# A convolution kernel stored by lag modulo 128, so that its Toeplitz rows are read in runs of 2 KB

## The chip, the core and the metric

The kernel runs on one core of a Trainium2 chip. The time is device microseconds (us) of one execution. The matrix engine is called PE in the profile and its weight loads PEld; VectorE is DVE, ScalarE is ACT, GpSimd is POOL, and SyncE, which issues most DMAs here, is SP. Five instruction streams run side by side and wait for each other on semaphores.

## The reference

Two branches work on the same sequence `x` of 2048 positions by 512 channels, and a gate mixes them:

```python
g = sigmoid((x * gate_w).sum(-1, keepdims=True))
a = attention(x, wqkv, wo)            # 32 heads of 16, full softmax over 2048 keys
b = ssm(x, ...)                       # see below
return g * a + (1 - g) * b
```

The second branch makes for each of the 512 channels a convolution kernel of 2048 taps from 128 complex modes, `K[d, l] = Re(sum_n C[d,n] * dt*B[d,n] * exp(dt*A[d,n] * l))`, and convolves the channel with it causally, `y[d, t] = sum_l K[d, l] * u[d, t - l]`, plus `u * Dskip`. (The reference does it with an FFT; the kernel does not.) Inputs and output are bf16.

## The kernel before, in words

**Attention** sets the rhythm. It is cut into 2048 score tiles of 128 keys by 512 queries. Three tiles make a group, 683 groups in all, numbered here from 0. For each group PE makes the scores (`SC<-Qm,KT`), ACT takes the exponential of them in one instruction (`ET<-SC`, 1536 columns wide), and PE multiplies the result with the values (`OA<-ET,VE`). From group 206 on, DVE takes one tile of many groups by a trick on the bits (`DZ<-SC`, then `DU`), so that ACT's instruction is 1024 columns wide there. Two score buffers, SC0 and SC1, alternate: PE can make the scores of one group while ACT works on the other.

**The second branch** is fitted into what the attention leaves of PE, DVE and the DMA queues, in this order:

- `params`: DVE makes powers of each mode's base, `L1`, `L2`, ..., by squaring. `POW` lists them.
- `tables`: for 8 slices (w) of 64 channels DVE makes two tables. The taps are a product of a 32-entry table `AT` and a 64-entry table `PL`, so that 32 x 64 = 2048 lags come from 96 entries. Thread `tables` may start after the mark "A" (the powers for `AT`), and needs "B" (those for `PL`) from its middle on.
- `kgen`: PE multiplies the tables (`MB<-PL,AT`, 2048 small matmuls), DVE moves the taps to `Ks`, and SP stores `Ks` to DRAM (`gm_kd<-Ks`). A slice is stored by 4 DMAs of 64 KB, one for each 16 channels.
- `relay`: `x` is transposed and written to DRAM as `xr`, in 16 planes (position modulo 16).
- `cloads`: for each of the 32 units of 16 channels SP loads the weights `WT` (4 DMAs of 256 KB from `gm_kd`) and the inputs `U` (2 DMAs of 284 and 288 KB from `gm_xr`). A row of `WT` is a Toeplitz row: row p + 1 is the same taps as row p, one lag further. Three buffers of each take turns.
- `convs`: 128 matmuls for each unit (`MB<-U,WT`): for 16 channels, 8 blocks of 128 lags. The weights of one matmul are 32 values per partition, taken from `WT` with a step; four matmuls lie side by side in four column strips of the array. DVE moves the result to `Ys`.
- `turn`: after two units, matmuls with a 0/1 matrix `sel` (`MB<-sel,Ys`) bring the result from 32 rows per channel back to positions.
- `gate`: the 44 small sums of the gate, in three parts of 12, 16 and 16, with matmuls of a single column (`MB<-gwT,xT`).
- `projs`: the projections of the attention (`MB<-Wv,xT`, `MB<-xT,Wk`, `MB<-xT,Wq`).

All of these share one bank of PSUM, `MB`, and lock it in turn.

**What sets the order.** A planner (`Sched`) runs when the kernel is built: threads offer their next piece with an estimated cost, and the piece that fits in before the next exponential is written into the engines' streams. It also puts in matmuls with zeros (`OA<-wm`, `SC<-wm`, `MB<-wm`) where PE would do too little. So any change of the work of one thread can shift the pieces of all others; on the chip each engine then works strictly in the order written.

Of the kernel before, what the change touches and what calls it, by code (L numbers as in the profile page):

```python
# [28 lines left out]
NPAD = 16  # L29
VB = (S + NPAD) * 16  # L30
# [53 lines left out]
POW = (1, 2, 4, 8, 16, 32, 48, 256, 512, 1024)  # L84
# [373 lines left out]
def declare(nc, es):  # L458
# [60 lines left out]
    for m in (4, 8, 512, 1024):  # L519
        sb(f"F{m}", 3 * D)  # L520
# [118 lines left out]
def record(nc, p, B, ins):  # L639
# [453 lines left out]
    def params():  # L1093
# [23 lines left out]
        for m in (4, 8):  # L1117
            yield from square(f"L{m}", f"L{m // 2}")
            yield from factor(f"F{m}", f"L{m}", key(f"L{m}"))
        for k, m in enumerate((16, 32)):  # L1120
            yield from square(f"L{m}", f"L{m // 2}")
            yield from factor("FF", f"L{m}", key(f"L{m}"), 3 * D * k)
        yield from fmul("L48", 1, "L16", key("L16"), "L32", key("L32"))
        yield from factor("FF", "L48", [(B["L48"], (0, "m"))], 6 * D)
# [49 lines left out]
    def tables():  # L1174
        AB, BS, FF = B["AB"], B["BS"], B["FF"]
        yield ("AFTER", "A")
        for w in range(8):
# [40 lines left out]
    dma("SP", lambda e: e.dma_start(kd.dram(S * 16, [[VB, 32], [1, 256]]), wm(0, [[1, 256]], 0, 32)), [(wm, 0)], [(kd, "z")], c=.6, lat=3)  # L1218

    def kgen(w):  # L1220
# [4 lines left out]
        for b in range(2):  # L1225
# [14 lines left out]
            op("DVE", lambda v, b=b: v.tensor_copy(ks(8 * b, [[16, 64], [1, 8]]), MB(0, [[1, 64], [64, 8]])), ky, [(ks, b, w)], c=.62)  # L1240
            sch.unlock("MB")
        sch.mark(f"kg{w}")
        for j in range(4):
# [1 line left out]
            dma("SP", lambda e, j=j: e.dma_start(kd.dram((4 * w + j) * VB, [[1024, 32], [1, 1024]]), ks(0, [[1, 1024]], 32 * j, 32)),
                [(ks, 0, w), (ks, 1, w)], [(kd, 4 * w + j)], c=.6, lat=3)
# [25 lines left out]
    def cloads():  # L1272
        yield ("AFTER", "xr")
        yield ("AFTER", CLAT)
        for x in range(NU_):
            v = x // UPV
            wt, ut = B[f"WT{v % NWT}"], B[f"U{x % NU}"]
            if x % UPV == 0:
# [3 lines left out]
                nb = 16 // WSP  # L1282
                for i in range(WSP):
                    yield ("SP", .65)
                    pc, sub = divmod(i, WSP // PC)
                    bigload(lambda e, pc=pc, sub=sub, i=i, wt=wt, v=v: e.dma_start(wt(NT * 16 * (PC * nb * sub + pc), [[NT * 16 * PC, nb], [1, NT * 16]]),
                                                                   kd.dram(v * VB + (16 // PC * pc + nb * sub) * 128 * 16, [[16, P], [128 * 16, nb], [1, NT * 16]])),
                            [(kd, v), (kd, "z")], [(wt, i, v)], 2 * NT * 16 * nb * P / 1000)
# [376 lines left out]
```

## Time and profile before

| | us |
|---|---|
| median of 3 timed runs | 792.45 (790.75 to 793.37) |
| the profiled execution, its own time | 790.26 |
| its span, first to last instruction | 788.5 |
| ACT busy in it | 764.4 |
| DVE busy | 698.6 |
| PE busy (ends of matmuls are modelled) | 706.7 |
| granted PE clock, mean | 0.992 |

The page gives busy times, the chain of work that ended last, and groups of instructions; the trace can also be asked for stretches of time (busy time of each engine, granted clock, DMA share) and for an engine's instructions in order of time, with the idle time ahead of each in brackets and what ended it. "issue" means that the engine waited for nothing that the profile shows. In DMA listings q1 is the queue of the data transfers and q8 and q14 carry instructions to the engines.

### The profile page before, as it was taken

To read this page: it belongs to the slowest core of one execution; us is meant where nothing else is said; L and a number is where in the kernel's file an instruction comes from. 1 tells how busy PE (TensorE), PEld (TensorE's weight loads), DVE (VectorE), ACT (ScalarE), POOL (GpSimd) and SP (SyncE) were. 2 spreads that over 40 slices of the span, in tenths; PEclk is the share of its full clock that TensorE was granted. 3 is DMA by queue.
4 is the path that set the end of the run, shared out by engine and by line. 5 is a ranking of instruction groups with operands and counts; after the bars stand their busy time and mean duration, and the time that the engine had idled before them with its cause. 6 is when DMAs were issued, how large, how long until landed. Compare 5 with 4: busy or idle time off the path is not lost.

```text
span 788.5 us, 31097 instructions
## 1 busy us (share of the span) xinstructions
PE 706.7 (90%) x14262; PEld 323.0 (41%) x14262; DVE 698.6 (89%) x1078; ACT 764.4 (97%) x694; POOL 11.9 (2%) x21
## 2 busy tenths in 40 slices
PE   6778777899899989999999999999999999998996
PEld 2323322454454544434444444444444444442221
DVE  5799999999899978878797988999989999999995
ACT  5999999999999999999999999999999999999995
POOL 4000000000000000000000000000000000000000
PEclk8999999999999999999999999999999999999999
DMA  9463000000100036003665555477554556304011
GB/s 213 84 127 63 9 5 20 24 25 26 30 25 26 26 100 162 13 19 86 171 176 157 150 160 166 143 196 207 159 163 131 145 167 173 88 7 124 32 35 35
DMA packets 125923, 76.22 MB, mean 97 GB/s; under 512 B 34240, under 2 KB 116576, under 8 KB 125792
## 3 DMA queue, kind: packets, MB, share of 16 engines
q1 hardware_dynamic: 123776, 73.05, 35.1%
q8 instruction: 112, 1.84, 1.0%
q10 hardware_dynamic: 2016, 1.18, 0.7%
q14 instruction: 19, 0.16, 0.1%
HBM read 59.12 MB, written 10.63 MB: 88 GB/s over the span
## 4 chain that ended last, share of the span: by engine, by line
ACT 84%; PE 12%; DVE 2%; POOL 1%; issue 1%; ACTq 0%; POOLq 0%
ACT ET L949 84%; PE SC L655 5%; PE OA L655 4%; PE MB L655 3%; POOL VE L723 1%; DVE DZ L985 1%; DVE OT L1020 0%; DVE DZ L996 0%; DVE Ys L1331 0%; ACT fo L1627 0%; DVE sel L1305 0%; DVE KT L749 0%; DVE YJ L1353 0%; ACT ea L1098 0%; DVE OnT L1039 0%
## 5 line engine op out<-in xcount | busy, mean ns | idle before, releaser
L949 ACT ACTIVATE ET<-SC 128x1024 bf16<-128x1024 f32 (+1 forms) x683 | 756.4, 1456 | 6.3 <-PE SC L655 5.1
L655 PE MATMUL SC<-Qm,KT 32*128 32x512 bf16 x2048 | 277.9, 385 | 63.8 <-ACT ET L949 58.7
L985 DVE TENSOR_SCALAR DZ<-SC 128x512 uint16<-128x512 f32 x384 | 255.8, 684 | 41.4 <-PE SC L655 38.9
L655 PEld LDWEIGHTS SC<-Qm,KT 32*128 32x128 bf16 x2048 | 71.4, 91 | 244.7 <-ACT ET L949 209.7
L655 PE MATMUL OA<-ET,VE 128*32 128x512 bf16 x1664 | 166.0, 391 | 0.2 <-ACT ET L949 0.2
L655 PE MATMUL OA<-wm 128*32 128x512 bf16 (+3 forms) x742 | 156.8, 366 | 1.7 <-DVE wm L706 1.2
L655 PEld LDWEIGHTS MB<-U,WT 128*32 128x32 bf16 x4096 | 91.4, 153 | 32.3 <-issue 22.6
L655 PE MATMUL MB<-U,WT 128*32 128x128 bf16 (+7 forms) x4096 | 103.3, 229 | 1.5 <-issue 1.5
L655 PEld LDWEIGHTS OA<-ET,VE 128*32 128x32 bf16 x1664 | 42.5, 93 | 93.2 <-issue 91.7
L996 DVE TENSOR_SCALAR DZ<-DZ 128x2048 uint16<-128x2048 uint16 x96 | 65.6, 683 | 7.9 <-PE OA L655 7.7
L655 PE MATMUL MB<-PL,AT 128*32 128x64 bf16 (+1 forms) x2048 | 68.9, 278 | 0.1
L996 DVE TENSOR_SCALAR DU<-DZ 128x2048 uint16<-128x2048 uint16 x96 | 64.5, 685 | 0.5
L655 PEld LDWEIGHTS MB<-PL,AT 128*32 128x32 bf16 x2048 | 56.1, 139 | 11.5 <-issue 5.7
L1043 DVE TENSOR_TENSOR PL<-PL,FF 128x2048 bf16<-128x2048 bf16 x48 | 56.2, 1217 | 0.3
L655 PEld LDWEIGHTS OA<-wm 128*32 128x32 bf16 (+2 forms) x742 | 40.3, 97 | 9.1 <-issue 7.3
L655 PE MATMUL OA<-DZ,VE 128*32 128x512 bf16 x384 | 38.0, 386 | 0.0
L655 PE MATMUL OA<-DZ,VS 128*32 128x512 bf16 x384 | 37.8, 383 | 0.0
L655 PE MATMUL OA<-DU,VS 128*32 128x512 bf16 x384 | 37.7, 383 | 0.0
L1020 DVE STREAM_TRANSPOSE OT<-OA 128x512 f32<-128x512 f32 x32 | 22.7, 709 | 5.2 <-PE OA L655 5.1
L1331 DVE CAST Ys<-MB 128x512 bf16<-128x512 f32 x32 | 21.7, 679 | 0.4 <-PE MB L655 0.2
L655 PE MATMUL MB<-Wv,xT 128*32 128x128 bf16 x1024 | 19.4, 219 | 0.0
L655 PEld LDWEIGHTS MB<-Wv,xT 128*32 128x32 bf16 x1024 | 16.7, 97 | 4.0 <-issue 1.1
(133 smaller groups left out, 449.2 us busy)
## 6 DMA issues: line engine op xcount, KB each, us to landing
WT<-gm_kd SPq DMA_DIRECT2D x128, 256.0 KB, 3.5
U<-gm_xr SPq DMA_DIRECT2D x32, 288.0 KB
U<-gm_xr SPq DMA_DIRECT2D x32, 284.0 KB
gm_xr<-Xp SPq DMA_DIRECT2D x4, 576.0 KB, 5.5
gm_kd<-Ks SPq DMA_DIRECT2D x32, 64.0 KB, 1.6
gm_yn<-YJ SPq DMA_DIRECT2D x2, 1024.0 KB, 4.8
Yl<-gm_yn SPq DMA_DIRECT2D x2, 1024.0 KB, 10.6
gm_qd<-Qs SPq DMA_DIRECT2D x15, 128.0 KB, 1.7
```

The costliest lines, as they stand in the source:

```text
L655: op("PE", lambda t: t.matmul(out(), lhsT(), rhs(), start=start, stop=stop, skip_group_check=True, **kw), R, W, c=c, lat=.15, a=a, cfg=cfg)
L723: op("POOL", lambda g, pi=pi: g.memset(VE(pi * 4 * VG, [[1, 4 * VG]]), 1.0), [(idb, 0)], [(VE, (pi, k)) for k in range(16)], c=2.3)
L949: op("ACT", lambda a: a.activation(ET(512 * e, [[1, 512 * n]]), sc(0, [[1, 512 * n]]), AF.Exp, scale=DH ** -0.5), [(sc, i, g) for i in ran ...
L985: op("DVE", lambda v: v.tensor_scalar(z.u16(512 * k, [[1, 512 * n]]), sc(512 * na, [[1, 512 * n]]), XS, XB, ALU.mult, ALU.add), [(sc, na + ...
L996: op("DVE", lambda v: v.tensor_scalar(t.u16(0, [[1, 2048]]), z.u16(0, [[1, 2048]]), float(STEP[k][0]), None, ALU.add), R, W, c=.07 + 2048 ...
L1020: op("DVE", lambda v: v.transpose(OT(512 * w, [[1, 512]]), OA(0, [[1, 512]])), [(OA, 0, b)], [(OT, w, b)], c=.64)
L1043: op(eng, lambda v: v.tensor_tensor(o(), a(), b_(), f), R, W, c=c)
L1331: op("DVE", lambda v_, ys=ys: v_.tensor_copy(ys(64, [[YW, NT // 4], [1, NJ]]), MB(0, [[NJ, NT // 4], [1, NJ]])), ky, [(ys, 0, x)], c=.62)
```

## The change

The taps of a channel block lie in DRAM in another order, and everything that makes or reads them follows.

- **Storage.** Before, lag l of 16 channels lay at `16 * l`. A Toeplitz row was read as 16 pieces of 512 B, from 16 places 4 KB apart, and rows lay 32 B apart. Now lag l lies at `256 * (l % 128) + 16 * (l // 128)`: 16 blocks of lags and 16 channels for one lag modulo 128 are 512 B in one place, and the next lag modulo 128 follows. A Toeplitz row of 16 lags is now 8 KB in one place; the four loads take 2 KB of each row. Rows lie 512 B apart.
- **Wrapping round.** Rows near the end run past lag modulo 128 = 127, so 16 more entries are stored behind: the first 16 again, moved on by one block of 128 lags. That is a second small store for each 16 channels, 32 in all (`gm_kd<-Ks 16x1x240`). The DMA of zeros at the start is reshaped for the same end.
- **Exponents traded.** The table with 64 entries now covers lags modulo 128 in a way that fits the storage, the one with 32 entries the rest: `POW`, the names `F...` and the two places in `params` are exchanged. The number and shape of the instructions stay, their order does not: the powers for `AT` and the mark "A" come first now, those for `PL` and "B" after them.
- **Weights of the convolution.** The 32 values per partition were 16 elements (32 B) apart in `WT`; now they are 128 elements (256 B) apart. The 32 result rows of a channel come out in another order (even and odd in place of two halves), and `sel` is made for that.

```diff
-VB = (S + NPAD) * 16
+VB = (P + 16) * 256
-POW = (1, 2, 4, 8, 16, 32, 48, 256, 512, 1024)
+POW = (1, 2, 16, 32, 64, 128, 256, 512, 1024, 1536)
...
-        sch.mark("B")
-        yield from square("LA", "L32", 0, 0)
+        yield from square("LA", "L2", 0, 0)
...
-        for m in (512, 1024):
+        for m in (32, 64):
             yield from square(f"L{m}", f"L{m // 2}")
             yield from factor(f"F{m}", f"L{m}", key(f"L{m}"), conj=True)
         sch.mark("A")
+        for m in (128, 256):
+            yield from square(f"L{m}", f"L{m // 2}")
+            yield from factor(f"F{m}", f"L{m}", key(f"L{m}"))
+        for k, m in enumerate((512, 1024)):
...
+        sch.mark("B")
...
-            op("DVE", lambda v, b=b: v.tensor_copy(ks(8 * b, [[16, 64], [1, 8]]), MB(0, [[1, 64], [64, 8]])), ky, [(ks, b, w)], c=.62)
+            op("DVE", lambda v, b=b: v.tensor_copy(ks(8 * b, [[16, 16], [256, 4], [1, 8]]), MB(0, [[4, 16], [1, 4], [64, 8]])), ky, [(ks, b, w)], c=.62)
...
+            yield ("SP", .6, 2)
+            dma("SP", lambda e, j=j: e.dma_start(kd.dram((4 * w + j) * VB + P * 256, [[1024, 4], [256, 4], [1, 240]]), ks(16, [[256, 4], [1, 240]], 32 * j, 4)),
+                [(ks, 0, w), (ks, 1, w)], [(kd, ("x", 4 * w + j))], c=.6, lat=3)
...
-                    bigload(lambda e, pc=pc, sub=sub, i=i, wt=wt, v=v: e.dma_start(wt(NT * 16 * (PC * nb * sub + pc), [[NT * 16 * PC, nb], [1, NT * 16]]),
-                                                                   kd.dram(v * VB + (16 // PC * pc + nb * sub) * 128 * 16, [[16, P], [128 * 16, nb], [1, NT * 16]])),
-                            [(kd, v), (kd, "z")], [(wt, i, v)], 2 * NT * 16 * nb * P / 1000)
+                    bigload(lambda e, n=n, i=i, wt=wt, v=v: e.dma_start(wt(n * i, [[1, n]]), kd.dram(v * VB + n * i, [[256, P], [1, n]])),
+                            [(kd, v), (kd, ("x", v)), (kd, "z")], [(wt, i, v)], 2 * n * P / 1000)
...
-                           lambda g=g, c=c, wt=wt: wt(512 * (nb - 1 - g) + NT * hf + c, [[16, 32]]),
+                           lambda g=g, c=c, wt=wt: wt(16 * (nb - 1 - g) + NT * hf + c, [[128, 32]]),
```

**How the order moves.** The counts of instructions on ACT, DVE and POOL are the same as before, and so are their shapes but for `Ks<-MB`. PE has 20 more matmuls, all with zeros. From group 289 to the end the streams of PE are the same in kind and order; the planner's shift lies ahead of that. The first place is SP around the first load of `WT`. Before (`Ks_145` and `Ks_146` are the two buffers of taps, `U_150` and `WT_147` the first buffers of inputs and weights):

```order
L1245 DMA gm_kd<-Ks_145 32x1024 x4
L1286 DMA WT_147<-gm_kd 128x4x256 x4
L1295 DMA U_150<-gm_xr 128x1x1152
L1295 DMA U_150<-gm_xr 128x1x1136
L1286 DMA WT_148<-gm_kd 128x4x256 x2
L769 DMA Qm<-gm_qd 16x512 x4
L1286 DMA WT_148<-gm_kd 128x4x256 x2
```

Now, at the same place:

```order
L1244 DMA gm_kd<-Ks_145 32x1024
L1247 DMA gm_kd<-Ks_145 16x1x240
L1461 DMA gm_qd<-Qs 128x512
L1244 DMA gm_kd<-Ks_145 32x1024
L1247 DMA gm_kd<-Ks_145 16x1x240
L1287 DMA WT_147<-gm_kd 128x1024 x4
L1295 DMA U_150<-gm_xr 128x1x1152
L1295 DMA U_150<-gm_xr 128x1x1136
L1287 DMA WT_148<-gm_kd 128x1024 x2
L768 DMA Qm<-gm_qd 16x512 x4
L1287 DMA WT_148<-gm_kd 128x1024 x2
```

Each store of taps has a small one behind it, and each load of weights has the same size in 128 runs where it had 512. The order of `WT`, `U` and `Qm` among each other is the same.

The second place is PE where the gate's single-column matmuls stand. Before, the first two parts of the gate (14 pieces of 8 matmuls) run together in groups 203 to 226, ahead of the last `kgen`; the end of the thinnest stretch, groups 216 to 219:

```order
L655 MATMUL SC<-Qm,KT 128x512
L655 MATMUL OA<-wm 128x512
L655 MATMUL SC<-Qm,KT 128x512 x2
L655 MATMUL OA<-ET,VE 32x512 x4
L655 MATMUL SC<-Qm,KT 128x512 x3
L655 MATMUL MB<-gwT,xT 128x1 x8
L655 MATMUL MB<-wm 32x448 x4
L655 MATMUL SC<-Qm,KT 128x512 x3
L655 MATMUL MB<-gwT,xT 128x1 x8
L655 MATMUL MB<-wm 32x448 x4
L655 MATMUL SC<-Qm,KT 128x512 x3
L655 MATMUL OA<-ET,VE 32x512 x4
```

Now the last `kgen` runs straight on to group 221, the gate's first part stands in groups 230 to 239, and two units of the convolution (groups 242 to 248) come ahead of its second part (250 to 262) and third (264 to 276). The end of the first part:

```order
L654 MATMUL SC<-Qm,KT 128x512 x3
L654 MATMUL MB<-gwT,xT 128x1 x8
L654 MATMUL MB<-wm 32x448 x4
L654 MATMUL SC<-Qm,KT 128x512 x3
L654 MATMUL SC<-wm 32x512 x8
L654 MATMUL SC<-Qm,KT 128x512 x3
L654 MATMUL OA<-ET,VE 32x512 x4
L654 MATMUL SC<-Qm,KT 128x512
L654 MATMUL OA<-wm 128x512
L654 MATMUL SC<-Qm,KT 128x512 x2
L654 MATMUL OA<-ET,VE 32x512 x4
L654 MATMUL OA<-DZ_61,VE 32x512 x4
L654 MATMUL MB<-U_150,WT_147 32x128 x4
```

So the stretch of single-column matmuls is cut in two, with convolution matmuls between. The second of the two (to group 263) ends with the same rows as the stretch before.

More of the change, by code (lines that the diff above doesn't have):

```diff
@@ L28 @@
 NJP = NJ + JX
-NPAD = 16
-VB = (S + NPAD) * 16
+VB = (P + 16) * 256
 HALF_PI = math.pi / 2
@@ L518, in declare @@
     sb("BS", 4 * 2 * D)
-    for m in (4, 8, 512, 1024):
+    for m in (32, 64, 128, 256):
         sb(f"F{m}", 3 * D)
@@ L1116, in params @@
         op("DVE", lambda v: v.tensor_copy(BS(0, [[1, 4 * D]]), ZW(0, [[1, 4 * D]])), zk, [(BS, 0)], c=1.15)
[L1117 to L1124, printed above, removed]
-        sch.mark("B")
-        yield from square("LA", "L32", 0, 0)
+        yield from square("LA", "L2", 0, 0)
         yield from square("LA", "LA", 2 * D, 0)
         yield from fmul("LA", 1, "LA", [(LA, 0)], "LA", [(LA, 2 * D)], 2 * D, at=4 * D)
-        yield from square("L256", "LA", 0, 2 * D)
+        yield from square("L16", "LA", 0, 2 * D)
         al = [(LA, 0), (LA, 2 * D), (LA, (4 * D, "m"))]
-        yield from fmul("AB", 3, "LA", al, "L256", key("L256"), conj=True, at=8 * D, t=("LT1", "LT2"))
-        for k, (x, xk, n, at) in enumerate(((LA, al, 3, 0), (B["L256"], key("L256"), 1, 6 * D))):
+        yield from fmul("AB", 3, "LA", al, "L16", key("L16"), conj=True, at=8 * D, t=("LT1", "LT2"))
+        for k, (x, xk, n, at) in enumerate(((LA, al, 3, 0), (B["L16"], key("L16"), 1, 6 * D))):
             c = .07 + n * .28
@@ L1142, in params @@
         sch.mark("A")
+        for m in (128, 256):
+            yield from square(f"L{m}", f"L{m // 2}")
+            yield from factor(f"F{m}", f"L{m}", key(f"L{m}"))
+        for k, m in enumerate((512, 1024)):
+            yield from square(f"L{m}", f"L{m // 2}")
+            yield from factor("FF", f"L{m}", key(f"L{m}"), 3 * D * k)
+        yield from fmul("L1536", 1, "L512", key("L512"), "L1024", key("L1024"))
+        yield from factor("FF", "L1536", [(B["L1536"], (0, "m"))], 6 * D)
+        sch.mark("B")
     AT, PL, ct1 = [B["AT0"], B["AT1"]], [B[f"PL{k}"] for k in range(NPL)], B["ct1"]
@@ L1184, in tables @@
             ak = [(at, "one"), (at, 0)]
-            for m, n in ((8, 512), (16, 1024)):
+            for m, n in ((8, 32), (16, 64)):
                 f = B[f"F{n}"]
@@ L1198, in tables @@
             pk = [(pl, 0)]
-            for m, n in ((4, 4), (8, 8)):
+            for m, n in ((4, 128), (8, 256)):
                 f = B[f"F{n}"]
@@ L1217, in record @@
     kd = B["kd"]
-    dma("SP", lambda e: e.dma_start(kd.dram(S * 16, [[VB, 32], [1, 256]]), wm(0, [[1, 256]], 0, 32)), [(wm, 0)], [(kd, "z")], c=.6, lat=3)
+    dma("SP", lambda e: e.dma_start(kd.dram(P * 256 + 240, [[VB, 32], [256, 16], [1, 16]]), wm(0, [[16, 16], [1, 16]], 0, 32)), [(wm, 0)], [(kd, "z")], c=.6, lat=3)
     def kgen(w):
@@ L1281, in cloads @@
                     yield ("AFTER", f"cv{UPV * (v - NWT + 1) - 1}")
[L1282 removed]
+                n = 4096 // WSP
                 for i in range(WSP):
                     yield ("SP", .65)
[L1285 to L1288 removed]
+                    bigload(lambda e, n=n, i=i, wt=wt, v=v: e.dma_start(wt(n * i, [[1, n]]), kd.dram(v * VB + n * i, [[256, P], [1, n]])),
+                            [(kd, v), (kd, ("x", v)), (kd, "z")], [(wt, i, v)], 2 * n * P / 1000)
             if x >= NU:
@@ L1302, in record @@
     Ys, YJ = [B[f"Ys{k}"] for k in range(NYS)], [B["YJ0"], B["YJ1"]]
-    op("POOL", lambda g: g.iota(sid(0, [[1, 4 * NT]]), [[-1, NT], [32, 4]], base=0, channel_multiplier=-1, allow_small_or_imprecise_dtypes=True), [], [(sid, 0)], c=.2)
+    op("POOL", lambda g: g.iota(sid(0, [[1, 4 * NT]]), [[-PC, NT], [32, 4]], base=0, channel_multiplier=-1, allow_small_or_imprecise_dtypes=True), [], [(sid, 0)], c=.2)
     for k in range(PC):
-        op("DVE", lambda v, k=k: v.tensor_scalar(sel(4 * NT * k, [[1, 4 * NT]]), sid(0, [[1, 4 * NT]]), 1.0 - NT * (PC - k), None, ALU.is_equal), [(sid, 0)], [(sel, k)], c=.15)
+        op("DVE", lambda v, k=k: v.tensor_scalar(sel(4 * NT * k, [[1, 4 * NT]]), sid(0, [[1, 4 * NT]]), k - 31.0, None, ALU.is_equal), [(sid, 0)], [(sel, k)], c=.15)
     def zeros():
```

## The prediction

> **What bounds the kernel now.** I read the page's busy times first, then its chain of waits, then where ACT was idle. The page's rows for the span, for the chain by engine and by line, and for the costliest group:
>
> ```profile
> PE 706.7 (90%) x14262; PEld 323.0 (41%) x14262; DVE 698.6 (89%) x1078; ACT 764.4 (97%) x694; POOL 11.9 (2%) x21
> ...
> ACT 84%; PE 12%; DVE 2%; POOL 1%; issue 1%; ACTq 0%; POOLq 0%
> ...
> L949 ACT ACTIVATE ET<-SC 128x1024 bf16<-128x1024 f32 (+1 forms) x683 | 756.4, 1456 | 6.3 <-PE SC L655 5.1
> ```
>
> ACT is busy for 764.4 of 788.5 us, and ahead of its 683 exponentials it was idle for 6.3 us in all. The change leaves those instructions as they are, in number and width. So there is a floor: what the change can win is part of these 6.3 us, and it can lose wherever PE is late with scores for ACT. The other 18 us lie at the start and the end, which the change does not touch.
>
> So the next question is what made up the 6.3 us. ACT in order of time, the rows that carry a wait of the middle (start, length, idle time before it in brackets):
>
> ```profile
> 300.38 4.76 ACT L949 ACTIVATE ET<-SC 128x1024 bf16<-128x1024 f32 x5 [0.20 <-PE SC L655]
> 305.55 2.12 ACT L949 ACTIVATE ET<-SC 128x1024 bf16<-128x1024 f32 x2 [0.41 <-PE SC L655]
> 308.17 1.02 ACT L949 ACTIVATE ET<-SC 128x1024 bf16<-128x1024 f32 x1 [0.49 <-PE SC L655]
> 309.56 2.79 ACT L949 ACTIVATE ET<-SC 128x1536 bf16<-128x1536 f32 x2 [0.37 <-PE SC L655]
> ...
> 386.54 4.77 ACT L949 ACTIVATE ET<-SC 128x1024 bf16<-128x1024 f32 x5 [0.27 <-PE SC L655]
> 392.25 8.93 ACT L949 ACTIVATE ET<-SC 128x1024 bf16<-128x1024 f32 x8 [0.93 <-PE SC L655]
> ...
> 541.58 47.19 ACT L949 ACTIVATE ET<-SC 128x1024 bf16<-128x1024 f32 x48 [0.36 <-PE SC L655]
> 589.84 3.03 ACT L949 ACTIVATE ET<-SC 128x1024 bf16<-128x1024 f32 x3 [1.07 <-PE SC L655]
> ```
>
> Two kinds. The first four (1.47 us) lie in the gate's stretch. The last four (2.63 us) lie among the convolutions. Before 280 us there is none. The first kind, by stretches of 2 us (PEclk is the granted clock):
>
> ```profile
> 304.00:306.00 2.00, 2.00 (x22) 0.90 (x21) 1.97 (x5) 1.59 (x3) 0.00 (x0) 0.74 0.57 151
> 306.00:308.00 2.00, 2.00 (x19) 0.34 (x15) 1.13 (x2) 1.60 (x2) 0.00 (x0) 0.50 0.90 238
> 308.00:310.00 2.00, 2.00 (x26) 0.99 (x23) 1.80 (x3) 1.47 (x2) 0.00 (x0) 0.91 0.97 221
> ```
>
> The clock was halved for about 3.4 us at the end of the gate's single-column matmuls, where PE has little to do; scores then came late. The waits of 0.41, 0.49 and 0.37, 1.27 us together, are its price.
>
> The second kind: the four "issue" steps of the chain of waits among the convolutions, then PE in order of time at the last of them, then what the DMA queues moved around it (one listing before 586 us, one after), and the page's row for the whole span:
>
> ```profile
> 385.21 0.56 issue
> ...
> 390.22 0.73 issue
> ...
> 540.46 0.66 issue
> ...
> 588.11 1.04 issue
> ...
> 587.46 0.65 PE L655 MATMUL MB<-U,WT 128*32 128x80 bf16 x25
> 589.15 0.33 PE L655 MATMUL MB<-U,WT 128*32 128x96 bf16 x7 [1.04 <-issue]
> ...
> q1 hardware_dynamic: 1316, 0.66, 46.4%
> ...
> q1 hardware_dynamic: 707, 0.35, 69.4%
> q8 instruction: 1, 0.02, 4.4%
> ...
> q8 instruction: 112, 1.84, 1.0%
> ```
>
> PE stopped for 1.04 us between two matmuls of one set of four (25 is no multiple of four), where nothing is left to wait for but its own next instructions. From 580.8 to 586 us the instruction queue moved nothing while weights ran through; one packet came between 586 and 588, just ahead of the stop. The other three steps stand right ahead of the waits at 386.54, 392.25 and 541.58. The 112 packets for 2 x 14262 instructions of PE make 255 for each. My reading: PE's instructions come over the same DMA engines, 256 at a time, and behind loads of `WT` and `U` a packet comes too late. The profile shows this order of events, not the cause.
>
> **The change, part by part.** The sum is made against the profiled execution's own 790.26 us. The median of the timed runs is 792.45, so 2.2 us are added at the end.
>
> *Weights with a step of 256 B.* No row has that step. The nearest, loads of 32 columns by group, and one run of the convolution:
>
> ```profile
> L655 PEld LDWEIGHTS MB<-U,WT x4096: 135/157/180, 357.0 to 706.7; 128*32 128x32 bf16 x196
> L655 PEld LDWEIGHTS MB<-PL,AT x2048: 131/137/162, 144.0 to 338.7; 128*32 128x32 bf16 x187
> L655 PEld LDWEIGHTS OA<-ET,VE 128*32 128x32 bf16 x1664 | 42.5, 93 | 93.2 <-issue 91.7 <-ACT ET L949 0.5 <-DVE OT L1020 0.5
> 581.82 0.54 PEld L655 LDWEIGHTS MB<-U,WT 128*32 128x32 bf16 x28 [0.23 <-issue]
> ```
>
> A step of 32 B (`WT`) has a median of 157 ns, a step of 128 B (`AT`) 137, packed columns a mean of 93. So a step costs about 50 ns, and four times the step costs no more. I take 256 B as the same: 0 us. Below: if the step cost nothing, PE would gain time in which it waits for ACT anyway, 0 us. Above: 28 loads take 0.54 us, less 0.16 for the last one, so a set of four takes 0.38 / 6 = 63 ns. Twice that is 64 us more over 1024 sets. The cover is PE's own waiting among the convolutions, from 395 to 700 us:
>
> ```profile
> PEld SC L655 <- ACT ET L949: 66.2, 158, 1.2
> PE SC L655 <- ACT ET L949: 12.7, 42, 0.7
> ```
>
> 66 us of cover for some 56 us (28 of the 32 units lie there) would do on average, but the sets lie unevenly; with a quarter uncovered it would be +15 us.
>
> *Loads of 2 KB runs.* Bytes and number of DMAs stay:
>
> ```profile
> WT<-gm_kd SPq DMA_DIRECT2D x128, 256.0 KB, 3.5
> ```
>
> Nobody waits for the data: the page has no wait of PE for `WT`. What they hold up is instruction packets. Two stretches, the first with weights in 512 B runs, the second with inputs `U` in runs of 2.2 KB:
>
> ```profile
> 584.50:586.00 1.50, 1.50 (x51) 0.98 (x51) 1.50 (x4) 1.50 (x3) 0.00 (x0) 1.00 1.12 327
> 381.00:383.00 2.00, 2.00 (x67) 1.22 (x59) 0.73 (x2) 2.00 (x3) 0.00 (x0) 1.00 0.51 193
> ```
>
> The last two columns are DMA share and GB/s. At a full share 512 B runs move 327 / 1.12 = 292 GB/s and long ones 193 / 0.51 = 378. A unit's 1.05 MB of weights then take 2.8 us of the queues at best, in place of 3.2 (at 327): 0.4 us sooner, or 0.8 if rate follows share. The four stops cost ACT 0.27, 0.93, 0.36 and 1.07. With 0.4 us off each, 0 + 0.5 + 0 + 0.7 = 1.2 are left, a gain of 1.4. I take 1.3, since 40 more PE instructions (20 matmuls with zeros and their loads) shift which packet meets which load. Bounds: all four gone, -2.6; or another stop as long as the longest, +1.1.
>
> [...]
>
> *The gate moved.* The first two parts of the gate now stand apart, with two thin stretches in place of one, the second ending in the same rows as before. One halved clock costs 1.27 us. I take one again: 0. Bounds: none, -1.3; two, +1.3. The other work that moves ahead of group 289 (the last `kgen`, two units of the convolution, projections) stays the same in sum and falls where PE waits for ACT now, between 60 and 280 us:
>
> ```profile
> PEld SC L655 <- ACT ET L949: 71.0, 137, 1.0
> ```
>
> *32 more small stores.* SP issues four stores of taps in 1.7 us and four `Qm` loads behind them:
>
> ```profile
> 243.29 1.26 SPq L1245 DMA_DIRECT2D gm_kd<-Ks  x3
> 244.59 1.82 SPq L769 DMA_DIRECT2D Qm<-gm_qd  x4
> ...
> 285.45 1.70 SPq L1245 DMA_DIRECT2D gm_kd<-Ks  x4
> 287.25 2.05 SPq L1286 DMA_DIRECT2D WT<-gm_kd  x4
> ```
>
> At 0.42 us each, four more put `Qm`, loaded a block (21 groups) ahead, 1.7 us later: hidden, 0. Without that cover it would be 1.7 us for each of the three blocks whose `Qm` stands right behind such stores, +5. The exchanged exponents and `Ks<-MB` in another shape are DVE's, on which ACT does not wait ahead of group 206: 0.
>
> Sum: 790.3 + 0 - 1.3 + 0 + 0 = 789.0 as a profiled execution, 791.2 as a median.
>
> **The rivals.**
>
> - *Slow weights.* Loads at 256 B take twice as long: 790.3 + 15 + 2.2 = 807. For it: a step costs 50 ns already. Against: 32 and 128 B do not differ. It decides from about 100 ns for a set of four, where the cover runs out.
> - *A rougher middle.* Both thin stretches lose their clock (+1.3) and no stop goes away, or one more comes (+1.1): 792.7, as a median 794.9. For it: the same rows that halved the clock before now come twice near enough. Against: thin stretches elsewhere kept the clock.
> - *Nothing changes.* The stops do not hang on the length of the runs: an instruction packet gets in after a few runs of any length, or it is the loads of `U`, which stay as they are, that hold it up. For it: `U` stands behind every load of `WT`. Against: ahead of the longest stop `U` was issued only as the packet came:
>
> ```profile
> 582.56 1.46 SPq L1286 DMA_DIRECT2D WT<-gm_kd  x3
> ...
> 586.46 2.17 SPq L1295 DMA_DIRECT2D U<-gm_xr  x2
> ```
>
>   Then 790.3, as a median 792.4. [...]
> - *All of it.* The four stops and the halved clock go: 790.3 - 2.6 - 1.3 = 786.4, as a median 788.6. For it: 0.8 us off each load would end two stops and most of a third. Against: the thin stretches are two.
>
> **How the numbers follow.** Chances: forecast 0.43, nothing changes 0.19, all of it 0.15, a rougher middle 0.14, slow weights 0.09. This kernel's runs differ by 0.3%, about 2.4 us, so that is what can be told from no change. Faster than 790.1: nearly all of "all of it" and a quarter of the forecast, 0.25. Slower than 794.8: slow weights, and two thirds of the rougher middle with a little from the others, 0.20. Same: 0.55. The range is 788.0 to 796.5: it takes in all but slow weights and the far edge of the best case.
>
> **What would show it.** Right: `MB<-U,WT` loads with a median near 137 to 160 ns; "issue" steps of the chain among the convolutions shorter or fewer, with the waits behind them; ACT idle ahead of its exponentials for about 5 us; a landing time of `WT` below 3.5 us. Wrong: loads of 200 ns and more with ACT waiting for scores in each unit of the convolution; a mean granted clock below that of before (0.992); ACT waits near a store of taps.

## The result and the profile after

The changed kernel takes 813.86 us in the median (811.65 to 814.96, 4 runs), the kernel before 791.6 (790.33 to 793.37) beside it: a ratio of 1.0276, with a 95% interval of 1.0242 to 1.0310. It is slower, by 22 us, where 791.2 was forecast.

The page of the changed kernel: busy times, the chain by engine, and the groups that answer to those shown of before (behind each `x` count: busy us, mean ns of one | idle time ahead and its cause), then the landing time of `WT`:

```profile
PE 737.8 (91%) x14282; PEld 364.6 (45%) x14282; DVE 723.3 (89%) x1078; ACT 788.8 (97%) x694; POOL 11.2 (1%) x21
...
ACT 67%; PE 27%; DVE 4%; POOL 1%; issue 1%; ACTq 0%; POOLq 0%
...
L948 ACT ACTIVATE ET<-SC 128x1024 bf16<-128x1024 f32 (+1 forms) x683 | 780.9, 1454 | 8.0 <-PE SC L654 5.9
...
L654 PEld LDWEIGHTS MB<-U,WT 128*32 128x32 bf16 x4096 | 133.0, 204 | 26.4 <-issue 22.4
...
L995 DVE TENSOR_SCALAR DZ<-DZ 128x2048 uint16<-128x2048 uint16 x96 | 80.4, 838 | 7.7 <-PE OA L654 7.4
...
WT<-gm_kd SPq DMA_DIRECT2D x128, 256.0 KB, 3.1
```

The same groups on the page of the kernel before, as far as the prediction does not show them:

```profile
L655 PEld LDWEIGHTS MB<-U,WT 128*32 128x32 bf16 x4096 | 91.4, 153 | 32.3 <-issue 22.6
...
L996 DVE TENSOR_SCALAR DZ<-DZ 128x2048 uint16<-128x2048 uint16 x96 | 65.6, 683 | 7.9 <-PE OA L655 7.7
```

The span grew by 24.6 us (788.5 to 813.1). ACT was busy for 24.4 us more (764.4 to 788.8), nearly all of it in the exponentials: 683 as before, of the same widths, busy for 780.9 us where it was 756.4. Ahead of them ACT was idle for 8.0 us, 1.7 more than before; elsewhere it was idle a little less. (The mean of one, 1454 ns, did not move. ACT's instructions lie over each other, 683 times 1454 ns being 993 us, so the mean does not tell.)

Busy time alone does not say why. Most exponentials start while the one before them still runs: 661 of 682 in the kernel before, 643 in the changed one. Where scores come a little late, this overlap shrinks (it is under 0.1 us, or a gap, for 35 before and for 72 in the changed kernel), and ACT can lose time without an idle gap. The starts and ends of single exponentials in the traces separate the two. Before, one of 1024 columns that started at least 0.1 us ahead of the end of its predecessor ended 917 ns behind it, whatever ran beside it (four in five between 915 and 918); one of 1536 columns 1343 ns. So 0.1 us of overlap is enough for the scores not to count. In the changed kernel, of those that started as early, the ones of 1024 columns with more than 16 convolution loads beside them take 1018 ns on the mean, the ones with none 914. Against the pace of before, the early ones lose 16.5 us in all (0.1 before, summed over both widths): there ACT works more slowly, with its scores at hand. All others, which started late or after a gap, lose 18.8 us (9.2 before): so up to some 10 us are late scores, most of them hidden in the busy time.

DVE works more slowly too: its step in place on `DZ`, which no edit touches, went from 683 to 838 ns.

ACT by stretches, ahead of the convolutions and among them. First the kernel before, then the changed one (length, busy time and number of instructions started, granted clock, DMA share, GB/s):

```profile
0.00:320.00 320.00, 309.45 (x240) 0.98 0.27 60
320.00:720.00 400.00, 395.65 (x396) 1.00 0.49 136
```

```profile
0.00:320.00 320.00, 310.25 (x242) 0.98 0.26 60
320.00:720.00 400.00, 393.63 (x369) 1.00 0.43 132
```

Up to 320 us nothing is lost. Then, in 400 us in which ACT hardly rests in either kernel, it gets through 369 instructions for 396: 393.63 / 369 = 1.067 us for each, and 395.65 / 396 = 0.999 before. The mix of widths is nearly the same (71 of the 368 exponentials have 1536 columns, and 76 of 395 before). The granted clock is 1.00 in both. The loss begins with the convolutions, so the experiments start at their weights.

### The profile page after: what moved, and what is told of

It is laid out like the page before. It is cut to its first block, busy times and chain, and to the rows that moved or that the text cites. A ratio compares the mean times of both kernels' runs of the same rounds, so it can differ in the third digit from the quotient of the medians.

```text
span 813.1 us, 31179 instructions
## 1 busy us (share of the span) xinstructions
PE 737.8 (91%) x14282; PEld 364.6 (45%) x14282; DVE 723.3 (89%) x1078; ACT 788.8 (97%) x694; POOL 11.2 (1%) x21
## 4 chain that ended last, share of the span: by engine, by line
ACT 67%; PE 27%; DVE 4%; POOL 1%; issue 1%; ACTq 0%; POOLq 0%
ACT ET L948 67%; PE MB L654 10%; PE SC L654 9%; PE OA L654 8%; DVE DZ L984 2%; POOL VE L722 1%; DVE DZ L995 1%; DVE OT L1019 0%; DVE Ys L1331 0%; DVE DU L995 0%; DVE YJ L1353 0%; ACT fo L1627 0%; DVE sel L1305 0%; DVE VE L758 0%; DVE KT L748 0%
## 5 line engine op out<-in xcount | busy, mean ns | idle before, releaser
L948 ACT ACTIVATE ET<-SC 128x1024 bf16<-128x1024 f32 (+1 forms) x683 | 780.9, 1454 | 8.0 <-PE SC L654 5.9
L984 DVE TENSOR_SCALAR DZ<-SC 128x512 uint16<-128x512 f32 x384 | 261.8, 703 | 41.5 <-PE SC L654 40.1
L654 PE MATMUL OA<-wm 32*128 32x512 bf16 (+3 forms) x758 | 157.4, 361 | 1.2 <-DVE wm L705 1.2
L654 PEld LDWEIGHTS MB<-U,WT 128*32 128x32 bf16 x4096 | 133.0, 204 | 26.4 <-issue 22.4
L654 PE MATMUL MB<-U,WT 128*32 128x120 bf16 (+7 forms) x4096 | 138.3, 257 | 1.5 <-issue 1.5
L995 DVE TENSOR_SCALAR DZ<-DZ 128x2048 uint16<-128x2048 uint16 x96 | 80.4, 838 | 7.7 <-PE OA L654 7.4
L995 DVE TENSOR_SCALAR DU<-DZ 128x2048 uint16<-128x2048 uint16 x96 | 72.0, 764 | 0.5
L654 PE MATMUL OA<-DZ,VS 128*32 128x512 bf16 x384 | 39.9, 383 | 0.0
```

What stands on the lines that cost most here:

```text
L654: op("PE", lambda t: t.matmul(out(), lhsT(), rhs(), start=start, stop=stop, skip_group_check=True, **kw), R, W, c=c, lat=.15, a=a, cfg=cfg)
L948: op("ACT", lambda a: a.activation(ET(512 * e, [[1, 512 * n]]), sc(0, [[1, 512 * n]]), AF.Exp, scale=DH ** -0.5), [(sc, i, g) for i in ran ...
L984: op("DVE", lambda v: v.tensor_scalar(z.u16(512 * k, [[1, 512 * n]]), sc(512 * na, [[1, 512 * n]]), XS, XB, ALU.mult, ALU.add), [(sc, na + ...
L995: op("DVE", lambda v: v.tensor_scalar(t.u16(0, [[1, 2048]]), z.u16(0, [[1, 2048]]), float(STEP[k][0]), None, ALU.add), R, W, c=.07 + 2048 ...
```

## Experiments

### Which edit it is: b256, a32

> The kernel before, with only the step of the weights set to 256 B (other taps of the same tile, so the convolution sums other products; storage, transfers and order are those of before). STEP: the whole loss without any other part of the change, 810 to 816 us, loads of 204 ns, DVE's in-place step above 0.8 us while loads run. RUNS: 790 to 793. PLACE: 790 to 793.

> The kernel after, with one number undone: the 32 weights of a matmul stand 32 B apart in the same tile, as before, not 256 B. (They are other taps than those asked for, so the convolution sums other products; number and size of all instructions and DMAs are those of the kernel after.) Theory STEP: weight loads that jump 256 B hold up the memory ports for ACT and DVE and are slow themselves; then the whole loss goes, 789 to 793 us, the loads are back at 157 ns and the in-place step of DVE (DZ from DZ) at 0.68 us. Theory RUNS (the 2 KB transfers into the tiles, or the planner's shift ahead of group 289, make the loss): stays at 810 to 815. Theory PLACE (tiles lie at other addresses, so that engines collide): stays at 810 to 815.

```diff
 before.py -> b256
-wt(512 * (nb - 1 - g) + NT * hf + c, [[16, 32]])
+wt(16 * (nb - 1 - g) + NT * hf + c, [[128, 32]])
 after.py -> a32
-wt(16 * (nb - 1 - g) + NT * hf + c, [[128, 32]])
+wt(512 * (nb - 1 - g) + NT * hf + c, [[16, 32]])
```

Measured: b256 816.85 us, ratio 1.0347 (1.0285 to 1.0409); a32 789.69 us, ratio 1.0015 (0.9978 to 1.0053). The pages of b256 and of a32:

```profile
PE 739.8 (91%) x14262; PEld 365.2 (45%) x14262; DVE 724.4 (89%) x1078; ACT 789.2 (97%) x694; POOL 11.8 (1%) x21
...
L655 PEld LDWEIGHTS MB<-U,WT 128*32 128x32 bf16 x4096 | 133.7, 205 | 24.7 <-issue 20.7
```

```profile
PE 711.7 (90%) x14282; PEld 324.2 (41%) x14282; DVE 697.8 (88%) x1078; ACT 765.0 (97%) x694; POOL 11.2 (1%) x21
...
L654 PEld LDWEIGHTS MB<-U,WT 128*32 128x32 bf16 x4096 | 91.5, 153 | 32.9 <-issue 23.0
```

The step alone, put into the kernel before, brings the whole loss (ACT busy 789.2); taken out of the changed kernel it takes the whole loss away (765.0). The storage, the 2 KB runs, the extra stores, the traded exponents and the moved pieces together come to no difference that can be told. So STEP holds as far as the times go (in b256 the loads take 205 ns for 153, DVE's step in place 826 for 683), and RUNS and PLACE do not. At which point the loads hold up ACT and DVE, no run shows.

### Is it the distance: a2, a64, a128, a192, a260

> The kernel after with a step of 128 B (other taps of the same tile). STEP with a cliff between 128 and 256 B, as the tables' matmuls (128 B) let expect, beside which DVE kept its 0.68 us: 789 to 794, loads of 137 to 157 ns. STEP as a price that grows with the step: about half way, 800 to 804. RUNS or PLACE: 810 to 815.

> The kernel after with a step of 260 B: as far as 256 B, but no power of two (other taps of the same tile). If the loss at 256 B comes from falling on the same part of the memory again and again: 789 to 794. If it comes from the distance alone: 810 to 815. RUNS or PLACE: 810 to 815.

> The changed kernel with the weights read without a step (32 elements side by side, 64 B in all); the weights are then the wrong elements of the same tile, so the convolution's values are wrong, its work is the same. [...] RIVAL (a load's length in the convolution is set by the instruction and what runs beside it, not by its elements' places): 150 to 160 ns.

> The changed kernel with the weights read at a step of 64 B; the weights are then the wrong elements of the same tile, so the convolution's values are wrong, its work is the same. [...] RIVAL (only at 128 B and above is a load slowed): 157 ns and 789 to 791 us.

> The changed kernel with the weights read at a step of 192 B; the weights are then the wrong elements of the same tile, so the convolution's values are wrong, its work is the same. [...] RIVAL (what counts is the distance in multiples of 64 or 128 B, so 192 B lies between 128 B and 256 B): loads 188 to 204 ns, ScalarE busy 775 to 789 us, 800 to 812 us.

```diff
 after.py, the 32 weights of a load
-wt(16 * (nb - 1 - g) + NT * hf + c, [[128, 32]])
+wt(512 * (nb - 1 - g) + 32 * c, [[1, 32]])                          # a2
+wt(1024 * (c // 4) + 4 * (nb - 1 - g) + c % 4, [[32, 32]])          # a64
+wt(2048 * (c // 8) + 8 * (nb - 1 - g) + c % 8, [[64, 32]])          # a128
+wt(16 * (nb - 1 - g) + NT * hf + c, [[96, 32]])                     # a192
+wt((16 * (nb - 1 - g) + c) % 64, [[130, 32]])                       # a260
```

| step | load, mean ns | ACT busy, us | DVE in place, ns | ratio to before |
|---|---|---|---|---|
| none (a2; the four loads of a set begin 64 B apart) | 97 | 764.5 | 683 | 0.9977 (0.9949 to 1.0005) |
| 32 B (a32) | 153 | 765.0 | 685 | 1.0015 (0.9978 to 1.0053) |
| 64 B (a64) | 154 | 763.9 | 683 | 0.9965 (0.9940 to 0.9990) |
| 128 B (a128) | 187 | 770.9 | 685 | 1.0112 (1.0055 to 1.0169) |
| 192 B (a192) | 151 | 763.5 | 683 | 0.9978 (0.9947 to 1.0008) |
| 256 B (changed) | 204 | 788.8 | 838 | 1.0276 (1.0242 to 1.0310) |
| 260 B (a260) | 159 | 764.3 | 684 | 0.9989 (0.9960 to 1.0019) |

The page of a192, then that of a128:

```profile
L654 PEld LDWEIGHTS MB<-U,WT 128*32 128x32 bf16 x4096 | 90.7, 151 | 33.7 <-issue 23.9
```

```profile
PE 725.9 (91%) x14282; PEld 346.2 (43%) x14282; DVE 698.9 (87%) x1078; ACT 770.9 (96%) x694; POOL 11.1 (1%) x21
...
L948 ACT ACTIVATE ET<-SC 128x1024 bf16<-128x1024 f32 (+1 forms) x683 | 763.0, 1394 | 11.9 <-PE SC L654 7.6
...
L654 PEld LDWEIGHTS MB<-U,WT 128*32 128x32 bf16 x4096 | 114.6, 187 | 29.2 <-issue 22.0
```

In all rows but the first the four loads of a set begin 2 B apart. It is not the distance: 260 B costs nearly what 32 B costs, and 192 B less than 128 B. Of the steps tried, 128 B and 256 B are dear, and 32, 64, 192 and 260 B are not. With 154 ns at 64 B the RIVAL of a64 held, that only at 128 B and above a load is slowed; 192 B (151 ns) shows that "above" does not hold either.

At 128 B, 798.70 us in the median lie between what a cliff and what a price that grows with the step had let expect, and the loss is of another kind. The loads are slow, DVE keeps its 685 ns, ACT waits 5.6 us more and is busy 6.6 us more. But here an exponential of 1024 columns that started early ends 917 ns behind its predecessor, as before (four in five between 914 and 918). So ACT is not slowed: these 12.2 us are late scores, in part hidden in the busy time. A load without a step takes 97 ns and gains the kernel nothing that can be told.

### Is 256 B dear everywhere: kg256, kg32

The lag generation has 2048 loads of the same shape, at 128 B. On their row of 137 ns the prediction had leant.

> The kernel before, with the weights that make the convolution kernel's lags (tables AT, 2048 loads ahead of the convolutions) read at a step of 256 B for 128 B; they are then the wrong elements of the same tile, so the lags are wrong, the work is the same. STEP (256 B hurts whichever matmul loads so): these loads go from a median of 137 ns to 180 ns and more, VectorE's and ScalarE's instructions beside them lengthen; with half as many loads as in the convolution, 3 to 12 us longer. RIVAL (the convolution's loads are slow for a reason of that place, its moving tile or its buffers): loads stay at about 137 ns and the time within 0.3%.

> The kernel before, with the same weights read at a step of 32 B for 128 B; they are then the wrong elements of the same tile, so the lags are wrong, the work is the same. HIDDEN (at 128 B these loads are as slow in themselves as the convolution's at 128 B, and the row of 137 ns that the prediction leant on is short because of what runs beside it): the loads become shorter than 137 ns, near 100 to 120 ns. RIVAL (in this place a load's length doesn't hang on its step between 32 and 128 B): 130 to 140 ns. Either way the time within 0.3%.

```diff
 before.py, kgen
-at(AN * (k // 2) + ch, [[CH, 32]])      # CH = 64 elements, 128 B
+at(ch, [[128, 32]])                     # kg256
+at(AN * (k // 2) + ch, [[16, 32]])      # kg32
```

Measured: kg256 788.71 us, ratio 0.9984 (0.9956 to 1.0011); kg32 790.54 us, ratio 1.0005 (0.9979 to 1.0030). The page of the kernel before, of kg256 and of kg32:

```profile
L655 PEld LDWEIGHTS MB<-PL,AT 128*32 128x32 bf16 x2048 | 56.1, 139 | 11.5 <-issue 5.7
```

```profile
PE 711.0 (90%) x14261; PEld 327.9 (42%) x14262; DVE 698.2 (89%) x1078; ACT 764.2 (97%) x694; POOL 11.9 (2%) x21
...
L655 PEld LDWEIGHTS MB<-PL,AT 128*32 128x32 bf16 x2048 | 59.8, 143 | 11.8 <-issue 5.7
```

```profile
L655 PEld LDWEIGHTS MB<-PL,AT 128*32 128x32 bf16 x2048 | 59.8, 147 | 11.2 <-issue 5.7
```

My theory STEP fell here: 256 B costs these loads 143 ns, 32 B 147 ns, 128 B 139, and ACT (764.2 us busy) and DVE (698.2) do not feel it. HIDDEN fell too: the loads did not become shorter at 32 B. A step of 256 B is not dear in itself. Two things were left that differ between the places. In the convolution the four loads of a set, one for each quarter of the array's columns, begin 2 B apart (four neighbouring channels), in the lag generation 32 B apart (channel 16 * j of four). And sets follow each other faster in the convolution: worked out from the runs of loads in the trace of the kernel before, some 80 ns apart on the mean (the most usual 63), for some 114 in the lag generation.

### The four loads of a set: s256, kgline

> The changed kernel, its weights still at a step of 256 B, but the four loads of a set (four channels, one for each quarter of TensorE's columns) begin 32 B apart from each other, as those of the lag generation do, where in the changed kernel they begin 2 B apart; they read the wrong lag blocks of the same tile, so the values are wrong, the work is the same. SET (it is the four loads of a set, which run at one time, that want the same line of memory; apart, they don't collide): loads 150 to 170 ns, VectorE's in-place step 685 to 720 ns, ScalarE busy 764 to 770 us, 0.995 to 1.008 of the kernel before. RATE (each load at 256 B is slow in itself; the lag generation hides it because its moving reads hold it to a set in 113 ns for 63 ns): loads still about 204 ns, ScalarE busy about 788 us, 1.025 to 1.035.

> The kernel before, with the weights of the lag generation at a step of 256 B, and the four loads of a set 2 B apart where they were 32 B apart; they are the wrong elements of the same tile, so the lags are wrong, the work is the same. SET: these loads now collide as the convolution's do, 165 ns and more for 143 with 256 B and 32 B apart; VectorE's and ScalarE's instructions beside them lengthen; over 512 sets the time grows by 2 to 12 us. RATE: nothing moves, 140 to 150 ns, time within 0.3%.

```diff
 after.py -> s256
-wt(16 * (nb - 1 - g) + NT * hf + c, [[128, 32]])
+wt(16 * ((nb - 1 - g + c % 4) % 8) + c, [[128, 32]])
 before.py -> kgline
-at(AN * (k // 2) + ch, [[CH, 32]])
+at(4 * (ch % 16) + ch // 16, [[128, 32]])
```

Measured: s256 787.88 us, ratio 0.9975 (0.9941 to 1.0010); kgline 841.96 us, ratio 1.0682 (1.0618 to 1.0747). The loads of a set begin 34 B apart in s256 (one block of lags and one channel; 222 B where the block wraps round). The page of s256, then that of kgline:

```profile
PE 710.1 (89%) x14281; PEld 318.5 (40%) x14282; DVE 697.5 (88%) x1078; ACT 765.1 (96%) x694; POOL 11.2 (1%) x21
...
L948 ACT ACTIVATE ET<-SC 128x1024 bf16<-128x1024 f32 (+1 forms) x683 | 757.2, 1450 | 11.9 <-PE SC L654 10.4
...
L654 PEld LDWEIGHTS MB<-U,WT 128*32 128x32 bf16 x4096 | 87.0, 146 | 36.0 <-issue 25.8
...
L995 DVE TENSOR_SCALAR DZ<-DZ 128x2048 uint16<-128x2048 uint16 x96 | 65.7, 685 | 9.5 <-PE OA L654 9.3
```

```profile
PE 732.3 (87%) x14261; PEld 347.5 (41%) x14262; DVE 751.2 (90%) x1078; ACT 814.9 (97%) x694; POOL 11.9 (1%) x21
...
L949 ACT ACTIVATE ET<-SC 128x1024 bf16<-128x1024 f32 (+1 forms) x683 | 807.0, 1544 | 6.0 <-PE SC L655 4.9
...
L655 PEld LDWEIGHTS MB<-PL,AT 128*32 128x32 bf16 x2048 | 81.0, 231 | 8.2 <-issue 6.6
```

SET holds both ways as far as the times go, RATE in neither; what of the memory the four want at one time, no run shows. With the same step of 256 B the convolution's loads fall to 146 ns once the four begin 34 B apart, and DVE and ACT get their times back. The lag generation's loads rise from 143 to 231 ns once the four begin 2 B apart. That its sets follow more slowly did not save it: the 51 us that it lost are four times what I had expected at most. A stretch in which lags are made, kernel before and kgline (length; busy time and number of instructions started of PE, PEld, DVE, ACT and POOL; granted clock, DMA share, GB/s):

```profile
140.00:240.00 100.00, 91.98 (x2035) 49.70 (x2036) 91.48 (x121) 100.00 (x76) 0.00 (x0) 1.00 0.09 25
```

```profile
140.00:240.00 100.00, 80.32 (x1543) 47.61 (x1542) 94.17 (x93) 100.00 (x59) 0.00 (x0) 0.98 0.07 20
```

ACT, the fourth, gets through 59 exponentials for 76 in the same time, all of 1536 columns, and is called busy all along. It is not short of scores: of the exponentials that started early, those with more than 16 loads of the lag generation beside them take 2032 ns on the mean, for 1343 before, and that makes up the whole growth of the busy time (50.6 us).

### Does it grow with the number of such sets, and is it all: half, half2, rot

> The changed kernel with half of the convolution's weights (the second and fourth quarter of each unit's channels) read at 256 B, the others at 64 B; the latter are then the wrong elements of the same tile, so values are wrong, the work is the same. ADDITIVE (each load at 256 B takes its own share of memory time from ScalarE and VectorE): ScalarE's busy time half way, 774 to 779 us, time half way, 797 to 804 us. RIVAL (only an unbroken train of such loads starves the other engines, short ones are absorbed): ScalarE busy below 769 us, time below 795 us.

> The changed kernel with the second and fourth quarter of each unit's channels read at 256 B, the others at 64 B; the latter are then the wrong elements of the same tile, so values are wrong, the work is the same. ADDITIVE: ScalarE's busy time half way, 774 to 779 us, time half way, 797 to 804 us. RIVAL (only an unbroken train of such loads takes time from the other engines): ScalarE busy below 769 us, time below 795 us.

> The changed kernel, data, storage and step of 256 B untouched; only the order in which each of the four channels of a set goes through its lag blocks differs: the first set has block 0 for all four, as it must, and in the seven behind it each channel is one block further than its neighbour, so that their loads begin 32 B apart or a multiple of it. Everything is computed. SET: seven of eight sets no longer collide; loads at a median near 150 ns with one in eight near 200, ScalarE busy 765 to 769 us, VectorE's in-place step below 705 ns, time 0.995 to 1.004 of the kernel before. RIVAL (the matmuls of a set then have different widths and no longer end together, or the colliding eighth still costs its part, 3 us, and more): 1.004 to 1.015.

```diff
 after.py -> half2
-wt(16 * (nb - 1 - g) + NT * hf + c, [[128, 32]])
+wt(16 * (nb - 1 - g) + c, [[128, 32]]) if c // 4 % 2 else wt(1024 * (c // 4) + 4 * (nb - 1 - g) + c % 4, [[32, 32]])
 after.py -> rot (everything computed)
-for g in range(nb):
+for t in range(nb):
     ...
     for j in range(4):
+        g = 1 + (t - 1 + j) % 7 if t else 0
```

`half` did not do what it was meant to: it chose by `q % 2`, and `q` is read when the matmul is written out, after the loop has ended at 3, so that all weights stayed at 256 B. It is a second measurement of the changed kernel: 814.01 us, ratio 1.0296 (1.0251 to 1.0341). half2, which chooses by `c`: 801.44 us, 1.0134 (1.0075 to 1.0193). rot: 792.68 us, 1.0035 (1.0003 to 1.0067). The pages of half2 and of rot:

```profile
L948 ACT ACTIVATE ET<-SC 128x1024 bf16<-128x1024 f32 (+1 forms) x683 | 769.5, 1436 | 10.0 <-PE SC L654 8.3
...
L654 PEld LDWEIGHTS MB<-U,WT 128*32 128x32 bf16 x4096 | 114.4, 181 | 30.2 <-issue 23.4
```

```profile
L948 ACT ACTIVATE ET<-SC 128x1024 bf16<-128x1024 f32 (+1 forms) x683 | 760.8, 1454 | 4.0 <-PE SC L654 3.1
...
L654 PEld LDWEIGHTS MB<-U,WT 128*32 128x32 bf16 x4096 | 96.4, 158 | 31.8 <-issue 23.4
...
L995 DVE TENSOR_SCALAR DZ<-DZ 128x2048 uint16<-128x2048 uint16 x96 | 68.7, 715 | 8.6 <-PE OA L654 8.3
```

With one colliding set in eight the exponentials are busy 4.4 us longer than before (760.8 less 756.4), with one in two 13.1, with all 24.5. Over 128, 512 and 1024 sets that is 34, 26 and 24 ns each: it grows with their number, and short trains are not absorbed. rot computes everything, keeps the changed data and the 256 B step, and loses about what its eighth part explains: 4.4 us of busy time, where an eighth of 24.5 is 3.1. DVE's step in place came out at 715 ns, above the 705 that SET allowed; why a single colliding set costs more than one in a train was not looked into. So the collision is the loss.

### Versions that avoid it: fix260, fix272

> The whole change, with two elements of padding behind every 128 of a granule, in the rows that are stored, in DRAM and in the tiles WT, so that the weights of the convolution step 260 B; the wrap-around is stored by two small transfers where there was one (32 more in all). Everything is computed. [...] RIVAL (the padding, the odd pitch of the rows and the extra small transfers cost something of their own): 2 to 6 us above the kernel before, with ScalarE idle ahead of the exponentials by more than 9 us or WT landing later than 3.3 us.

> The whole change, with one element of padding behind every 16 channels (a lag takes 17 places), in the rows that are stored, in DRAM and in WT, so that the weights of the convolution step 272 B; the wrap-around stays one transfer, unlike with the padding behind every 128 places. Everything is computed. STEP: loads of a set about 152 to 158 ns, VectorE's in-place step 685 ns, ScalarE busy about 764 us; without the second wrap transfer the time is that of the other steps that cost nothing, 0.995 to 1.000 of the kernel before. RIVAL (padding and the odd pitch cost something, whatever the number of small transfers): 1.002 to 1.007, ScalarE idle ahead of the exponentials 8 us and more.

The main lines of both edits, cut:

```diff
 after.py -> fix272 (17 places for the 16 channels of a lag, everything computed)
-VB = (P + 16) * 256
+VB = (P + 16) * 272
-ks(8 * b, [[16, 16], [256, 4], [1, 8]])
+ks(8 * b, [[17, 16], [272, 4], [1, 8]])
...
-ks(16, [[256, 4], [1, 240]], 32 * j, 4)
+ks(17, [[272, 4], [1, 255]], 32 * j, 4)
...
-wt(16 * (nb - 1 - g) + NT * hf + c, [[128, 32]])
+wt(17 * (nb - 1 - g) + c, [[136, 32]])
 after.py -> fix260 (2 places behind each 128; the wrap-around in two stores)
...
-wt(16 * (nb - 1 - g) + NT * hf + c, [[128, 32]])
+wt(16 * (nb - 1 - g) + NT * hf + c, [[130, 32]])
```

Measured: fix260 792.99 us, ratio 1.0036 (1.0014 to 1.0059); fix272 787.19 us, ratio 0.9964 (0.9931 to 0.9997). The page of fix272, then that of fix260:

```profile
L948 ACT ACTIVATE ET<-SC 128x1024 bf16<-128x1024 f32 (+1 forms) x683 | 756.3, 1441 | 7.7 <-PE SC L654 6.5
...
L654 PEld LDWEIGHTS MB<-U,WT 128*32 128x32 bf16 x4096 | 89.3, 150 | 32.3 <-issue 22.3
```

```profile
L948 ACT ACTIVATE ET<-SC 128x1024 bf16<-128x1024 f32 (+1 forms) x683 | 757.0, 1406 | 9.4 <-PE SC L654 8.2
...
L654 PEld LDWEIGHTS MB<-U,WT 128*32 128x32 bf16 x4096 | 98.4, 159 | 34.0 <-issue 25.6
```

Both have the exponentials' busy time of before (756.4). fix272 is 3.0% faster than the changed kernel by the ratios (0.9964 / 1.0276 = 0.970) and 0.4% faster than the kernel before, with an interval that just leaves out 1. fix260 came out 0.4% above before, as its rival said it might: ACT idle 9.4 us and waiting for scores. The length of its loads is not enough to explain that: a260 has the same 159 ns and stands at 0.9989. Whether the 32 further small stores do it was not taken apart.

## Why the prediction was wrong, step by step

- **"... four times the step costs no more. I take 256 B as the same: 0 us."** This term of the sum failed. It was the whole loss, 24.6 us of the span: b256 shows that the step alone brings it, a32 that without it nothing is lost. The term compared 32 B in the convolution (157 ns) with 128 B in the lag generation (137 ns), as if the step were all that differs. The four loads of a set begin 2 B apart in the one and 32 B apart in the other. In the convolution itself the answer at 128 B is 187 ns (a128), and at 256 B 204 ns. The row of 137 ns could not have told it: kg32 and kg256 show that in that place the length hardly hangs on the step (147, 139, 143 ns).
- **The floor.** "The change leaves those instructions as they are, in number and width. So there is a floor: what the change can win is part of these 6.3 us, and it can lose wherever PE is late with scores for ACT." The first half holds: ACT's busy time was 763.5 us or more in every version. The second half names only one of the two ways to lose. The kernel can also lose where ACT's own instructions become slower with their scores at hand, and that was some 16 us. I had taken the time of an instruction as its own property, where here it hung on what ran beside it too (DVE's step in place: 683 and 838 ns).
- **The upper bound** (loads twice as long, 64 us more of PE, 15 us of it uncovered). PE's weight loads were busy 41.6 us longer (91.4 to 133.0). ACT's idle time shows only 1.7 us of that, but with the lateness hidden in overlaps up to some 10 us came through, and 12 in a128, where ACT is not slowed. So as a price for late scores 15 us was a fair bound; 0 was too small, and the other way to lose was missing.
- **The rival "slow weights"**, 807 us with a chance of 0.09, had the right edit and a part of the mechanism. Its sign in the profile, "ACT waiting for scores in each unit of the convolution", did not come: from 320 to 760 us ACT waited for scores 15 times, 4.8 us in all (before: 6 times, 3.2 us). Loads of 200 ns and more did.
- **"Loads of 2 KB runs", -1.3 us.** `WT` landed in 3.1 us for 3.5, the 0.4 us sooner that I had worked out. But over all runs with loads of 256 KB the medians are 2.9 to 3.5 us with 2 KB runs and 3.3 to 3.6 with 512 B runs, so one pair proves little. Where no sets collide and nothing is padded (a2, a32, a64, a192, a260, s256), the ratios to before lie at 0.9965 to 1.0015, and all intervals but that of a64 reach 1, so a gain of that size is possible and not shown. Its mechanism is not borne out. The prediction quotes four "issue" steps; the chain of the kernel before has a fifth among the convolutions, and a32, with 2 KB runs and the same step of the weights, has four, longer in sum. The fifth of before, then those of a32, in the chain of waits:

```profile
475.29 0.42 issue
```

```profile
471.60 0.99 issue
...
527.29 1.23 issue
...
542.76 0.47 issue
...
548.78 1.41 issue
```

  That makes 3.41 us in five before and 4.10 us in four here; a64 has two, of 1.74 and 1.12 us. The stops come and go from kernel to kernel, and no run shows that longer runs of the loads shorten them. That they are instruction packets late behind loads stays an open reading.
- **The gate moved: 0.** In the changed kernel the clock stayed at 1.00 from 296 to 328 us and ACT had no wait there, so the 1.27 us of the halved clock did go, and are lost in the 24.6. The stores and exchanged exponents at 0 hold: a32 has them all and stands at 1.0015.

## What to carry to other kernels

When matmuls run side by side in column strips, look at what their weight loads read at one time. In this kernel a step of 256 B together with starts that lie 2 B apart was dear (24.6 us of the span, a ratio of 1.0276). A padding of one element per 16 (fix272, 0.9964) or another order of the accumulation (rot, 1.0035) took nearly all of it away. Where the busiest engine's own instructions could get slower beside the new work, idle time is no ceiling for the loss: here it was 6.3 us ahead of the exponentials, and they were busy for 24.5 us more. Where instructions overlap, late inputs can hide in busy time: in a128 they were 12.2 us, of which 5.6 show as idle time. Before a price is taken from a row with the same shape and step, look at what runs beside it and at where its neighbours start: at 256 B such loads took 143 ns in the lag generation (kg256) and 204 in the convolution.

## What the runs showed of the hardware

- Weight loads of TensorE slowed ACT and DVE here. DVE's step in place reads and writes only its own tile `DZ`, and takes 683 ns on the mean in the kernel before and 838 in the changed one; its step from the scores, `DZ<-SC`, went only from 684 to 703. In kgline its costliest step on the tables, beside the loads of the lag generation, went from 1217 to 1545:

```profile
L1043 DVE TENSOR_TENSOR PL<-PL,FF 128x2048 bf16<-128x2048 bf16 x48 | 56.2, 1217 | 0.3
```

```profile
L1043 DVE TENSOR_TENSOR PL<-PL,FF 128x2048 bf16<-128x2048 bf16 x48 | 70.7, 1545 | 0.3
```

  ACT's exponentials lost some 16 us to it in the changed kernel, and 50.6 in kgline. By their edits b256 and s256 differ from their partners in the places of PE's reads alone: from the kernel before to b256 DVE's step in place goes from 683 to 826 ns and ACT's busy time from 764.4 to 789.2 us, from the changed kernel to s256 from 838 to 685 ns and from 788.8 to 765.1 us. So in these runs PE's weight reads held up ACT and DVE. At which point ACT, which reads scores and writes `ET`, is held, no run separates.
- In these runs it came with both together, a step of 256 B and loads of one set that start 2 B apart (loads of 204 ns in the changed kernel, 205 in b256, 231 in kgline). With starts 30 B and more apart (kg256 143 ns, s256 146 ns, seven of eight sets in rot), or with a step of 32, 64, 192, 260 or 272 B (loads of 150 to 159 ns, DVE's step in place 683 to 685 ns), it did not come. At 128 B the convolution's loads are slow (187 ns), and ACT and DVE are not. Packed columns take 97 ns (a2, whose starts differ too) and a step of 32 B about 153. The length does not follow the distance: 187 and 204 ns at 128 and 256 B stand beside 151 at 192 B. What makes those two dear was not shown. Starts between 2 and 30 B apart, and steps above 272 B, were not tried.
- A colliding set cost 24 to 34 ns of ACT's busy time in the convolution, late scores included, and 50.6 us / 512 = 99 ns in the lag generation. Why it is dearer there stays open; the lag generation's moving operand is read with a step too (128 B), which no run varied.
